# Block-sparse attention and a multiplicative FFN on one core: a new order of all engines and loads, paced loads, and pairs of heads taken by twos

## The chip, the cores and the metric

One NeuronCore of a Trainium2 chip. The metric is the device time of one execution in microseconds. The kernel before has a median of 254.29 us (254.08 to 254.67, three runs). The times that the chip reports are above the span of the same execution (254.47 against 252.7 in the profiled run of before), so spans are compared with spans and times with times.

## The reference, cut to what matters

```python
B, H, S, D = 4, 8, 768, 64                       # block = 32, 24 blocks
scores = scale * q @ k.T                         # per head
scores = where(mask, scores, -1e9)               # band, first and last block, 3 random blocks a row
attn   = softmax(scores);  x = attn @ v          # 3072 tokens x 512 after the heads are joined
a = x @ w1;  b = x @ w2                          # 512 -> 1024
out = ((a * b) @ w3) @ w_out                     # 1024 -> 1024 -> 512
```

Both kernels compute the product of w3 and w_out once (64 matmuls of 512 columns) and then two stages per 512 tokens: 64 matmuls for a and b, 32 for the output. There are six such FFN units.

## The kernel before

The kernel is a list of tasks with a duration, dependences and buffers. A small scheduler at build time plays the list through with modelled times, decides which task each engine takes next, and the instructions are then written in that order. The traces show each engine taking its instructions in that order, so a late input holds up what stands behind it on the same engine (TensorE's wait of 0.90 us ahead of its first FFN matmul, shown in the prediction, is one case).

```python
LOADS = ("a01 v00 v01 o0 o1 30 a02 v02 31 32 a03 v03 33 34 35 36 37 "
         "10 20 11 21 12 22 13 23 p10 p11 p12 p13 ...")   # a: q,k  v: v  o: w_out  3: w3  1,2: w1,w2  p: q,k,v
PRM = dict(bias=0.4, ..., vprio=1.5, w3prio=10.0, ..., trb=8, units="tttt", ...)
# (cut)
    def pick(self, eng, cands, free):                  # next task of an engine
        t0 = min(c[0] for c in cands)
        near = [c for c in cands if c[0] <= t0 + PRM["near"]]
        return min(near, key=lambda c: (c[1].prio, c[0]))
# (cut) keys and queries of the first trb pairs of heads: transposed on TensorE; later pairs: by DMA
            if (b, pr) in by_pe:
                # 12 nc.tensor.transpose each for q and k, then one eviction
            else:
                # a copy on VectorE, then nc.sync.dma_start(..., transpose=True)
# (cut) a tile of attention: 4 score matmuls, exp, mask multiply, 8 value matmuls
            prev_s = add(f"S {sk}", {PE: 0.216}, sc, ..., mode="S")
            exps.append(add(f"E {m} {j}", {ACT: 0.97}, ...))
# (cut) the FFN waits for x, which is transposed by DMA when all four pairs of a 256-token block are done
```

Two score buffers in PSUM limit how far TensorE can run ahead of ScalarE's exp. TensorE is kept busy at the start with matmuls on zeros ("spare"), so that its clock is up (in the trace of before the full clock is granted from 5.3 us on).

The softmax here doesn't subtract the row's maximum and nothing guards it: scores larger than these inputs give would overflow.

## Time and profile before

| | before |
|---|---|
| time, median | 254.29 us |
| span of the profile | 252.7 us |
| busy: TensorE, ScalarE, VectorE | 95%, 74%, 69% |
| first exp / first FFN matmul | 10.3 / 61.7 us |
| end of the last matmul to end of span | 4.0 us |

How to read it: with TensorE at 95% the question is not which engine is slow, but where TensorE has no useful work. The prediction below counts that. "Granted clock" is the share of its full clock that TensorE had.

### The profile page before, as it was taken

The page shows a single profiled execution, that of the slowest core. Times are in us where ns is not written, and L with a number is a line of the kernel's source. Part 1 is how long each engine was busy: PE and PEld are TensorE (multiplying, and loading weights), DVE is VectorE, ACT ScalarE, POOL GpSimd, SP SyncE. Part 2 cuts the span into 40 slices and gives each one's busy share as a digit, 9 for nine tenths or more (in the row PEclk, how much of TensorE's full clock was granted, in tenths as well). Part 3 has the DMA queues.
Part 4 walks back from the last instruction along what each step waited for, and adds up shares of the span by engine and source line. Part 5 has one row for each costly group of instructions (what it writes and reads, how often), then busy time and mean ns, then how long its engine had stood idle before and what let it go on. Part 6 is the DMA issues. An engine that isn't in the chain of part 4 may idle for free.

```text
span 252.7 us, 6330 instructions
## 1 busy us (share of the span) xinstructions
PE 240.6 (95%) x2647; PEld 130.5 (52%) x2689; DVE 174.9 (69%) x305; ACT 186.4 (74%) x231; POOL 44.9 (18%) x73
## 2 busy tenths in 40 slices
PE   7989999997999999999999999999999999999993
PEld 5554655664555455455455445555555554444441
DVE  5696698899699897988856776878777754312320
ACT  3685788897889898889888888788988862323321
POOL 8635455444421360000000000000000000000000
PEclk9999999999999999999999999999999999999998
DMA  7999999999997899994142020231201223022013
GB/s 174 171 205 207 208 210 194 164 199 167 177 173 99 104 144 194 184 242 86 34 110 101 4 42 3 61 108 44 42 4 21 65 89 79 0 83 83 4 42 125
DMA packets 45793, 28.08 MB, mean 111 GB/s; under 512 B 27332, under 2 KB 40644, under 8 KB 45764
## 3 DMA queue, kind: packets, MB, share of 16 engines
q0 software_dynamic: 15872, 14.29, 38.2%
q1 hardware_dynamic: 29892, 13.38, 25.4%
q8 instruction: 21, 0.34, 0.6%
q14 instruction: 8, 0.07, 0.1%
HBM read 29.36 MB, written 6.29 MB: 141 GB/s over the span
## 4 chain that ended last, share of the span: by engine, by line
PE 86%; DVE 4%; DMA 4%; ACT 3%; issue 2%; SPq 0%
PE f L622 33%; PE f L642 17%; PE s L528 14%; PE o L551 14%; PE f L603 5%; DMA x<-xn 4%; PE o L397 2%; DVE e L538 2%; ACT e L534 2%; PE f L474 1%; PE f L591 1%; DVE xn L561 1%; ACT qkt L293 0%; DVE w3t L293 0%; SPq L574 0%
## 5 line engine op out<-in xcount | busy, mean ns | idle before, releaser
L534 ACT ACTIVATE e<-s 128x1024 bf16<-128x1024 f32 x144 | 139.6, 1025 | 13.5 <-PE s L528 12.8
L622 PE MATMUL f<-x,w 128*128 128x512 bf16 x359 | 90.4, 379 | 2.8 <-issue 1.0
L538 DVE TENSOR_TENSOR e<-e,mask 128x2048 bf16<-128x2048 bf16 x72 | 87.4, 1218 | 7.4 <-ACT e L534 7.1
L551 PEld LDWEIGHTS <-e 128*128 128x128 bf16 x1152 | 44.1, 97 | 22.9 <-DVE xn L561 6.5
L633 DVE TENSOR_TENSOR big<-f,a 128x512 bf16<-128x512 f32 x48 | 33.1, 689 | 32.0 <-PE f L622 24.9
L551 PE MATMUL o<-v,e 128*128 128x65 bf16 x1152 | 50.6, 194 | 0.8 <-DVE xn L561 0.4
L622 PEld LDWEIGHTS <-w 128*128 128x128 bf16 x384 | 32.4, 98 | 35.3 <-issue 6.7
L642 PE MATMUL f<-wf,big 128*128 128x512 bf16 x183 | 46.2, 380 | 0.9 <-issue 0.6
L630 ACT CAST a<-f 128x512 bf16<-128x512 f32 x48 | 28.2, 588 | 24.6 <-PE f L622 24.6
L528 PE MATMUL s<-qkt 64*128 64x256 bf16 x576 | 45.2, 272 | 0.7 <-ACT e L534 0.7
L528 PEld LDWEIGHTS <-qkt 64*128 64x128 bf16 x576 | 22.2, 94 | 27.5 <-issue 24.1
L642 PEld LDWEIGHTS <-big 128*128 128x128 bf16 x192 | 16.1, 98 | 17.3 <-issue 3.2
L293 ACT COPY ob<-f 128x512 f32<-128x512 f32 x20 | 11.7, 587 | 14.1 <-PE f L642 14.1
L561 DVE TENSOR_TENSOR xn<-o,rec 128x256 bf16<-128x256 f32 x48 | 20.4, 424 | 1.7
L559 DVE RECIPROCAL rec<-o 128x4 f32<-128x4 f32 x48 | 8.6, 179 | 17.3 <-PE o L551 17.3
L603 PE MATMUL f<-wo,w3t 128*128 128x512 bf16 x56 | 15.8, 380 | 0.6 <-issue 0.3
L331 POOL DMA_DIRECT2D qn<-in_q_dram x15 | 10.9, 727 | 18.9 <-DVE qs L483 5.3
L331 POOL DMA_DIRECT2D kn<-in_k_dram x15 | 10.8, 719 | 14.1 <-DVE qs L483 6.2
L331 POOL DMA_DIRECT2D vn<-in_v_dram x16 | 11.4, 716 | 8.2 <-DVE v L496 5.8
L397 PE MATMUL o<-zero 128*128 128x256 bf16 (+1 forms) x45 | 7.8, 331 | 1.5 <-DVE zero L394 1.5
L293 DVE COPY qkt<-f 128x768 bf16<-128x768 bf16 x13 | 7.1, 552 | 2.0 <-PE f L474 1.9
L603 PEld LDWEIGHTS <-w3t 128*128 128x128 bf16 x64 | 4.9, 98 | 5.0 <-issue 0.6
(54 smaller groups left out, 87.1 us busy)
## 6 DMA issues: line engine op xcount, KB each, us to landing
out_dram<-ob SPq DMA_DIRECT2D x24, 256.0 KB, 2.0
vn<-in_v_dram POOLq DMA_DIRECT2D x16, 192.0 KB, 7.8
qn<-in_q_dram POOLq DMA_DIRECT2D x15, 192.0 KB, 8.1
kn<-in_k_dram POOLq DMA_DIRECT2D x15, 192.0 KB, 8.1
big<-in_moe_w_dram POOLq DMA_DIRECT2D x8, 256.0 KB, 8.9
w<-in_moe_w_dram POOLq DMA_DIRECT2D x8, 256.0 KB, 9.7
wo<-in_moe_w_out_dram POOLq DMA_DIRECT2D x2, 512.0 KB, 9.4
q<-in_q_dram SPq DMA_DIRECT2D x1, 384.0 KB, 3.2
```

The costliest lines, as they stand in the source:

```text
L293: (nc.scalar.copy if t.eng == ACT else nc.vector.tensor_copy)(out, in_)
L331: t = add(name, {POOL: 0.73}, lambda t: nc.gpsimd.dma_start(out=out_of(), in_=src), deps=deps, writes=writes, kind="load", prio=seq[0])
L528: nc.tensor.matmul(s[:, h, k2 * QT:(k2 + 1) * QT], lhsT=z[64 * h:64 * h + 64, 1, kc * 128:(kc + 1) * 128], rhs=z[64 * h:64 * h + 64, 0, t3 ...
L534: exps.append(add(f"E {m} {j}", {ACT: 0.97}, lambda t, sk=sk, ek=ek, j=j: nc.scalar.activation(T(*ek)[:, j], T(*sk), AF.Exp, scale=1.0 / 8 ...
L538: tm = add(f"K {m}", {DVE: 1.23}, lambda t, ek=ek, t3=t3, kp=kp: nc.vector.tensor_tensor(T(*ek), T(*ek), mask[:, t3, kp:kp + 2, :].unsquee ...
L551: nc.tensor.matmul(o[:, qt, h, :], lhsT=e[:, j, h, lo:lo + 128], rhs=w[:, h, kc, :], start=kc == 0 and qt == 0 and h == 0, stop=kc == C - ...
L561: tx = add(f"xn {rk}", {DVE: 0.42}, lambda t, rk=rk, ok=ok, xk=xk, pr=pr: nc.vector.tensor_tensor(T(*xk)[:, :, 128 * pr:128 * pr + 128].re ...
L603: nc.tensor.matmul(T(*key), lhsT=T("w3t", i)[:, j, :], rhs=wo_sb[:, j, :], start=j == 0, stop=j == NF - 1)
L622: nc.tensor.matmul(T(*key), lhsT=w[:, c, f * 128:(f + 1) * 128], rhs=T(*xk)[:, c, :], start=c == 0, stop=c == 3)
L630: ta = add(f"a {i}{f}", {ACT: 0.58}, lambda t, ak=ak, key=ends["w1"][0]: nc.scalar.copy(T(*ak), T(*key)), deps=[ends["w1"][1]], reads=[end ...
L633: nc.vector.tensor_tensor(T(*hk)[:, 512 * (f % 2):512 * (f % 2) + 512], T(*key), T(*ak), op=ALU.mult),
L642: nc.tensor.matmul(T(*key), lhsT=T(*hk[f // 2])[:, 512 * (f % 2) + n * 128:512 * (f % 2) + (n + 1) * 128], rhs=wf_sb[:, f, :], start=f == ...
```

## The change

The stated intent is an order that holds up under DMA delays. The scheduler's durations and its model of the DMA rings are refitted, its weights and the order of loads are searched for the mean time over replays with random delays, and some structure changes with it. The core of the diff, with cuts:

```diff
-LOADS = ("a01 v00 v01 o0 o1 30 a02 v02 31 32 a03 v03 33 34 35 36 37 "
-         "10 20 11 21 12 22 13 23 p10 p11 p12 p13 "
+LOADS = ("a01 30 a02 31 a03 v00 v01 36 o0 o1 v02 v03 32 35 33 34 37 20 10 22 p10 13 12 11 21 p11 "
+         "p12 23 p13 p20 p21 p22 p23 p30 p31 p32 p33")
-PRM = dict(bias=0.4, bmask0=1.0, bmask=1.0, btc=0.5, near=0.12, soon=0.06, kprio=2.0, eprio=0.5, aprio=1.0,
-           hprio=1.0, vprio=1.5, w3prio=10.0, ebufs=4, both=0.25, fo="31", pcopy=4.0, trb=8, units="tttt",
+PRM = dict(bias=0.102, bmask0=0.628, bmask=0.149, btc=-0.719, near=0.137, soon=0.0, kprio=3.289, eprio=0.296,
+           aprio=1.064, hprio=0.884, vprio=2.486, w3prio=28.201, ebufs=4, both=0.328, fo='31', pcopy=4.0,
+           trb=6, lead=9, slow=1.08, xeach=0.036, late=1.597, early=0.596, xlate=1.0, units='tQQQ', nat=4,
 ... first q and k: in halves, q from SP and k from ACT, cast and transposed by halves ...
+    def gate(b, pr):            # loads of batches 2 and 3 wait for a softmax reciprocal 9 units earlier
+            GATE[at] = add(f"gate {at}", {POOL: 0.2}, lambda t, rk=rk: nc.gpsimd.tensor_copy(
+                gate_sb, T(*rk)[:, 0, 0]), reads=[rk], prio=seq[0])
 ... opening zeros 128 instead of 256 columns wide while the clock is low ...
-        rows = 64 if mode == "S" else 128
+        rows, n = 64 if mode == "S" else 128, 128 if cold else 256
 ... the last output tile in two halves ...
+            width = d_model if 4 * i + n < 4 * NU - 1 else d_model // 2
```

`trb=6` sends pairs 2 and 3 of batch 1 through DMA transposes; `units='tQQQ'` takes the pairs of batches 1 to 3 two at a time.

## The prediction

> **What bounds the kernel now.** I read the page's busy shares first. TensorE is busy 95% of the span, against 74% for ScalarE and 69% for VectorE, and the granted clock is full. In the busy tenths the reader is to see that PE's first slices are the only ones under 9 besides the last: whatever can still be won lies in the first 60 us or so, and at the very end.
>
> ```profile
> span 252.7 us, 6330 instructions
> PE 240.6 (95%) x2647; PEld 130.5 (52%) x2689; DVE 174.9 (69%) x305; ACT 186.4 (74%) x231; POOL 44.9 (18%) x73
> PE   7989999997999999999999999999999999999993
> ```
>
> Second, the chain that ended last, in order of time. It is PE nearly throughout, and its pieces give the price of each kind of PE work.
>
> ```profile
> 1.47 5.41 PE o L397 x31
> 7.38 0.81 ACT qkt L293
> 8.23 0.86 PE f L474 x24
> 10.32 3.78 ACT e L534 x4
> 14.12 1.23 DVE e L538
> ...
> 175.48 0.73 PE o L551 x24
> 176.21 0.86 PE f L622 x4
> ...
> 201.34 0.54 PE s L528 x8
> 201.89 0.97 PE f L642 x4
> ...
> 241.92 6.92 PE f L642 x32
> 248.86 0.59 ACT ob L293
> ```
>
> A 512-column FFN matmul is 6.92 / 32 = 0.216 us. A value matmul (line 551) is 0.73 / 24 = 0.030. Eight score matmuls (528) are 0.54, of which the work is four pairs at 0.107 and the rest a change of array mode; the four FFN matmuls just after scores take 0.97 instead of 0.86, so leaving that mode costs another 0.1. Narrow transposes (474) are 0.86 / 24 = 0.036.
>
> Third, PE's timeline and its waits: where PE was not doing useful work.
>
> ```profile
> 1.47 5.41 PE L397 MATMUL o<-zero 128*128 128x256 bf16 x31 [1.47 <-DVE zero L394]
> 6.81 0.53 PE L474 MATMUL f<-ident,qn 128*64 128x128 bf16 x12
> ```
>
> ```profile
> PE f L622 <- DMA x<-xn: 0.9, 1, 0.9
> ```
>
> The 31 matmuls on zeros keep the clock up until data comes. But ScalarE had cast q by 3.92 + 0.83 = 4.75 us (its timeline), and the transposes started only at 6.81: the zeros ran 1.9 us too long. The last line is the first FFN matmul, which waits for transposed activations until 61.7 us.
>
> I add up the useful PE work from instruction counts and those prices: 640 FFN-size matmuls x 0.216 = 138.2; 1152 value matmuls x 0.0305 = 35.1; 288 score pairs x 0.107 = 30.8; 64 w3 transposes x 0.055 = 3.5; 192 narrow transposes x 0.028 = 5.4 between mode changes; masks 2.4; about 174 mode changes x 0.096 = 16.7. Sum 232.2. The span of 252.7 therefore holds 20.5 us without useful work. Where: 47.4 us of useful work stand ahead of the first FFN matmul at 61.7, so 14.3 are lost by then (6.8 before the first transpose, 1.6 for 14 later zero matmuls, 5.9 in waits). From 61.7 to PE's last matmul, ending 248.7, 187.0 us hold 184.8 of work: 2.2 lost, within the error of my prices. The tail from 248.7 to 252.7 is 4.0: cast, store, landing. 14.3 + 2.2 + 4.0 = 20.5.
>
> **What the Trainium skill says.** "TensorE: Matmul & The Clock Gate", under "What's actually happening", says that the array starts at half clock and needs about 3.4 us of activity to be released. The trace agrees: the 256-column zeros start 0.213 apart until 5.3 us and 0.109 after. So some zeros are needed, and their length should fit the time, not exceed it. "TensorEngine Tiling (Array Packing)" says, under "Key Properties", that changing the tiling mode drains the engine; the trace has 0.1 us per change, as above. "DMA: Bandwidth & Descriptors", under "Issuing engines are not separate DMA queues", says that transfers started from several engines run on the same 16 DMA engines and interleave. The trace agrees: while loads run, one activation transpose took 9.25 us on the chain; the fastest took 2.4.
>
> ```profile
> 52.34 9.25 DMA x<-xn
> ```
>
> ```profile
> DMA to landing us min/median/max: 2.4/4.0/10.5
> ```
>
> So pacing the loads can shorten those, but issuing the first k load from ScalarE only saves issue time (0.46 us).
>
> **The change part by part.** No arithmetic of the result changes; instructions move. The comparison of the programs' orders gives the counts.
>
> 1. Start. First q and k come in halves on two queues, are cast and transposed by halves, and the transposes take both heads at once. The first score group then needs only the first halves. Zeros before the first transposes fall to 30, now of 128 columns: cold at half of 0.213, 30 x 0.107 = 3.2 us, ending near 4.5. First useful work near 4.7 instead of 6.8: about -2.1. The first exp comes some 4 us earlier (near 6.2 instead of 10.3).
>
> 2. Zeros later: 26 after the first transposes instead of 14; some 26 x 0.1 = 2.6 against 1.6: +1.0. They stand where PE waits anyway, so they are a sign that 5 to 17 us stays thin.
>
> 3. Before the first value matmul the new order puts 9.3 us of useful work, the old 5.8: three more score tiles, more transposes, all masks. But v of the first pair is now seventh in the load queue and w_out eleventh. In the trace a 192 KB load lands about 1.0 us after the one before, a w3 block 1.2 and half of w_out 3. From the first landing at 6.5 us I estimate v at 16 and the second half of w_out at 22 to 23 (before: 9.7 and 16.7). ScalarE's chain gives the same time: ten exps at 0.93 plus eight evictions at 0.7 from 6.2 us end near 21. First w3·w_out product near 22.5 with 12.9 us of work done: 9.6 lost, against 10.0 before (18.9 with 8.9 done). So the earlier start gains only about 0.4 by this point; most is spent waiting for ScalarE and for v and w_out.
>
> 4. From there to the first FFN matmul the old order lost 14.3 - 10.0 = 4.3 us. The new order has 33.2 us of PE work there against about 25 exps x 0.92 plus 6 us of evictions = 29 on ScalarE, so PE can be dense; and it has ten more value tiles after the last that the first FFN input needs. I give it 1.7 lost. Gain 2.6.
>
> 5. 60 fewer narrow transposes on PE (pairs 2 and 3 of batch 1 go through DMA, first pair by twos): 60 x 0.036 = 2.1. Score groups stay at 76, so mode changes hardly change. On the bound engine this counts in full: -2.1.
>
> 6. Steady part: PE was already dense. Pairs by two and gated loads cannot gain here; they only must not lose. I set 2.6 lost against 2.2: +0.4.
>
> 7. The last output is cast and stored in two halves: half a cast (0.59 / 2) and a little of the store: -0.4.
>
> Sum over the span: -0.4 (1 to 3) - 2.6 - 2.1 + 0.4 - 0.4 = -5.1. Corrected for how far my reading of part 3 may be too strict (the load estimate uses a contended queue; the truth may be a microsecond better), -5.5. 254.3 - 5.5 = 248.8 us.
>
> **Rivals.** First, ScalarE becomes the bound. The new order leaves 244 FFN-size matmuls after the last value matmul, the old 188: 52.7 us against 40.6. So attention must be done in about 185 us instead of 196, with 166 us of ScalarE busy time in it: 90%. For: scores sit in pairs with two PSUM buffers, and 144 exps in the row of groups have a mean of 1.025 us; PE runs in fixed order, so a late exp stalls everything behind it. A stall of 0.05 us at each of 53 score groups is 2.7 us: 251.5. Against: exps that follow each other start 0.92 to 0.97 apart (3.78 for four), so the real load is lower.
>
> Second, a load takes the place of the wait. w_out later in the queue, or the gates, which tie batches 2 and 3 to a softmax reciprocal nine units earlier (some 34 us at 2.5 us per score group of two tiles). A late w_out would cost 2 or 3 us in one place: 251. The gates have so much lead against 9 us of landing that I expect nothing.
>
> Third, everything fits: PE starts at 4.7 and is filled by 15 us, with the losses before FFN at 9 instead of 11.3. That gives 246.5.
>
> Fourth, the order gains on a mean over delays, but this chip's delays are small (before runs within 0.6 us), so the robustness is not seen: then only parts 1, 5 and 7 count, about -3: 251.3.
>
> **Range and chances.** Two per cent is 5.1 us, that is 249.2. My sum lies at the edge of it: the sure parts (fewer transposes, tail, start) are 3 us, the rest depends on how densely PE is filled between 15 and 60 us. I put the 80% range at 246.2 to 251.7; faster by over 2% at 0.57, within at 0.42, slower at 0.01, since nothing adds work to PE.
>
> **What the profile after would show.** Right: transposes on PE starting before 5 us; first exp before 7; first FFN matmul at 56 to 59 us; PE's slices at 9 from the third on; no wait for x or exp over 0.5 us. Step 3 wrong if value matmuls start well before 16 us or w3·w_out waits on w_out. The ScalarE rival shows as PE waits for exp at line 624 spread over 60 to 190 us and the eights in PE's slices there. If the first FFN matmul is still later than 60 us, step 4 is wrong and the time stays above 250. If the first FFN is at 57 and the time still over 250, the steady part lost what the start gained.

## More of the kernel before

A view that the prediction did not show looks at ScalarE, which feeds TensorE with exps: between 10 and 30 us it works 14.58 of 20 us (columns: stretch, its length, then busy time and instruction count of TensorE, of its weight loads, of VectorE, ScalarE and GpSimd, then granted clock, DMA share, GB/s).

```profile
10.00:30.00 20.00, 18.52 (x239) 10.64 (x238) 15.21 (x30) 14.58 (x19) 8.57 (x15) 1.00 1.20 205
```

## The result, and the profile after

The changed kernel takes 247.21 us (247.11 to 247.40, four runs) against 254.24 in the same rounds: ratio 0.9722, 95% interval 0.9705 to 0.9739. A ratio here is the mean time of one kernel's fast runs over that of the other's fast runs of the same rounds, so it is not quite the ratio of the medians. Three executions of the later rounds that are slow (605.87 us of the kernel before, 258.94 of `b_cut`, 257.41 of `a_prm`) are left out of the ratios.

The page of the changed kernel: the span is 7.3 us shorter, and TensorE's first slices are full.

```profile
span 245.4 us, 6319 instructions
PE 240.5 (98%) x2648; PEld 131.5 (54%) x2648; DVE 175.8 (72%) x308; ACT 185.6 (76%) x232; POOL 46.6 (19%) x82
PE   8999999999999999999999999999999999999994
```

The busy time of TensorE is nearly the same (240.5 against 240.6), but the sum hides that the trace of before lacks 42 matmul records (2647 of 2689) and that of after none. TensorE's waits in the whole of the trace after are one line, the memset ahead of the first zero matmul; before there were ten.

```profile
PE o L478 <- POOL zero L475: 1.1, 1, 1.1
```

TensorE's timeline after (start, length, engine, line of the kernel, what is written from what, count; in brackets the idle time before it and what ended it), at the same places as before: transposes begin at 4.56 instead of 6.81, value matmuls at 18.56 instead of 14.87, the first FFN matmul at 56.10 instead of 61.72.

```profile
1.11 3.38 PE L478 MATMUL o<-zero 128*128 128x128 bf16 x30 [1.11 <-POOL zero L475]
4.56 0.50 PE L564 MATMUL f<-ident,q0n 128*128 128x128 bf16 x3
...
18.56 0.89 PE L647 MATMUL o<-v,e 128*128 128x65 bf16 x24
...
56.10 1.46 PE L721 MATMUL f<-x,w 128*128 128x512 bf16 x6
```

ScalarE in the stretch shown above for before: 18.13 of 20 us instead of 14.58. Sixteen exps are done at 30 us instead of ten.

```profile
10.00:30.00 20.00, 19.83 (x285) 12.23 (x282) 18.89 (x37) 18.13 (x23) 8.87 (x15) 1.00 1.22 206
```

The chain at the end: the last matmuls and a cast of half the width, 0.37 us instead of 0.59.

```profile
237.98 3.92 PE f L745 x26
241.90 0.03 ACTq L343
241.92 0.04 issue
241.96 0.37 ACT ob L343
```

Where the 7.4 us of span (252.71 to 245.35) went, counted as in the prediction (useful work from the orders: 232.2 before, 230.1 after):

| stretch | before | after | gain |
|---|---|---|---|
| start to the first w3 w_out product: time without useful work | 19.52 - 8.9 = 10.6 | 22.21 - 12.9 = 9.3 | 1.3 |
| from there to the first FFN matmul | 42.20 - 38.5 = 3.7 | 33.89 - 33.2 = 0.7 | 3.0 |
| from there to the last matmul's end | 186.9 - 184.8 = 2.1 | 185.6 - 183.9 = 1.7 | 0.4 |
| tail | 4.05 | 3.63 | 0.4 |
| useful work | 232.2 | 230.1 | 2.1 |

The sum is 7.2; the rest is rounding of my prices. Of the two gains of 0.4, that of the tail is read off the traces; that of the row above it is within what the prices can be off.

### The profile page after: what moved, and what is told of

The parts are those of the page before. It is cut to its first block, busy times and chain, and to the rows that moved or that the text cites. A ratio compares the mean times of both kernels' runs of the same rounds, so it can differ in the third digit from the quotient of the medians.

```text
span 245.4 us, 6319 instructions
## 1 busy us (share of the span) xinstructions
PE 240.5 (98%) x2648; PEld 131.5 (54%) x2648; DVE 175.8 (72%) x308; ACT 185.6 (76%) x232; POOL 46.6 (19%) x82
## 4 chain that ended last, share of the span: by engine, by line
PE 95%; ACT 2%; DVE 1%; POOL 0%; issue 0%; ACTq 0%; POOLq 0%
PE f L721 35%; PE f L745 17%; PE s L624 16%; PE o L647 16%; PE f L702 6%; PE f L690 2%; PE f L555 1%; PE o L478 1%; PE f L528 1%; ACT e L630 1%; PE f L564 1%; ACT qkt L343 1%; DVE hot L509 0%; DVE hot L507 0%; DVE q0n L343 0%
## 5 line engine op out<-in xcount | busy, mean ns | idle before, releaser
L630 ACT ACTIVATE e<-s 128x1024 bf16<-128x1024 f32 x144 | 140.8, 1030 | 13.6 <-PE s L624 12.2
L721 PE MATMUL f<-x,w 128*128 128x512 bf16 x384 | 94.0, 379 | 0.0
L647 PEld LDWEIGHTS <-e 128*128 128x128 bf16 x1152 | 43.4, 97 | 17.5 <-issue 4.0
L647 PE MATMUL o<-v,e 128*128 128x65 bf16 x1152 | 49.0, 194 | 0.0
L745 PE MATMUL f<-wf,big 128*128 128x512 bf16 (+1 forms) x200 | 46.8, 371 | 0.0
L745 PEld LDWEIGHTS <-big 128*128 128x128 bf16 x200 | 17.5, 98 | 17.6 <-issue 2.1
L343 ACT COPY ob<-f 128x512 f32<-128x512 f32 (+1 forms) x19 | 10.7, 564 | 16.1 <-PE f L745 16.1
L702 PE MATMUL f<-wo,w3t 128*128 128x512 bf16 x64 | 16.5, 380 | 0.0
L456 POOL COPY gate<-rec 128x1 f32<-128x1 f32 x8 | 1.4, 180 | 70.7 <-DVE rec L655 70.6
L478 PE MATMUL o<-zero 128*128 128x128 bf16 (+2 forms) x56 | 7.6, 297 | 1.1 <-POOL zero L475 1.1
(59 smaller groups left out, 98.1 us busy)
```

Of the source, the lines that this page charges most:

```text
L343: (nc.scalar.copy if t.eng == ACT else nc.vector.tensor_copy)(out, in_)
L630: exps.append(add(f"E {m} {j}", {ACT: 0.915}, lambda t, sk=sk, ek=ek, j=j: nc.scalar.activation(T(*ek)[:, j], T(*sk), AF.Exp, scale=1.0 / ...
L647: nc.tensor.matmul(o[:, qt, h, :], lhsT=e[:, j, h, lo:lo + 128], rhs=w[:, h, kc, :], start=kc == 0 and qt == 0 and h == 0, stop=kc == C - ...
L702: nc.tensor.matmul(T(*key), lhsT=T("w3t", i)[:, j, :], rhs=wo_sb[:, j, :], start=j == 0, stop=j == NF - 1)
L721: nc.tensor.matmul(T(*key), lhsT=w[:, c, f * 128:(f + 1) * 128], rhs=T(*xk)[:, c, :], start=c == 0, stop=c == 3)
L745: nc.tensor.matmul(T(*key)[:, :width], lhsT=T(*hk[f // 2])[:, at:at + 128], rhs=wf_sb[:, f, cols], start=f == 0, stop=f == NF - 1)
```

## The experiments

Twelve kernels, each against the kernel before in five rounds. Three chips were used; a variant of the changed kernel is best set beside the changed kernel's ratio (0.9722 or 0.9705), and its span beside 245.3 to 245.4. Each profile is of one execution; where that one lies at the edge of a wide run, the text says so. First, the changed kernel once more: 247.09 us, ratio 0.9705 (0.9683 to 0.9727), span 245.3.

> The changed kernel once more, unaltered, as the measure for the others of these rounds. Both theories: 247.2, span 245.4.

### Is TensorE the bound, or ScalarE?

```diff
+                        if i == 2 and part == 0:
+                            nc.tensor.matmul(T(*key), lhsT=w[:, 0, f * 128:(f + 1) * 128], rhs=T(*xk)[:, 0, :],
+                                             start=True, stop=True)
```

> The changed kernel with 16 superfluous 512-column matmuls in the third FFN unit, 3.45 us of TensorE work in the steady part, all orders else the same. Theory 1 (TensorE is the bound there, without slack): +3.4, 250.6, and ScalarE's idle time grows. Theory 2 (ScalarE paces it, TensorE hides some): under +2.

250.68 us against 247.09 in the same rounds: +3.6; span 249.5, +4.1. All 3.45 us of added work show, and a little more (the extra matmuls are closed groups of their own, overwritten at once; the profiled execution is the slowest of the five). ScalarE's busy time between 100 and 160 us falls from 55.10 to 52.80: there it had followed, not led. So the first rival of the prediction is refuted for this stretch, that of the third FFN unit; ahead of the first FFN matmul it was not tested in this way.

```profile
100.00:160.00 60.00, 60.00 (x746) 32.52 (x743) 52.71 (x92) 55.10 (x66) 10.20 (x18) 1.00 0.90 134
```

```profile
100.00:160.00 60.00, 59.14 (x716) 32.34 (x726) 50.64 (x87) 52.80 (x63) 10.94 (x19) 1.00 0.93 135
```

The first line is the changed kernel, the second the one with the extra matmuls (42 matmul records are missing from that trace as from that of before, so its PE column is a little low).

### The start alone, in the old order

```diff
+    zeros = [t for t in log if t.name == "spare"][16:31]
     for t in log:
-        t.go(t)
+        if not any(t is z for z in zeros):
+            t.go(t)
```

> The kernel before with 15 of its 31 opening zero matmuls left out, every other instruction in the same order. Theory 1 (the zeros overran by 1.9 us, but what follows soon waits for the k cast, ScalarE and loads): first transposes near 5.0 instead of 6.8, first exp near 8.9 instead of 10.3, first FFN matmul 0.6 to 1.2 us earlier, time 253.3. Theory 2 (the start counts in full, since TensorE is the bound): 252.3. Theory 3 (all of it is absorbed by later waits): 254.2.

Transposes begin 1.8 us earlier, the first exp 0.8 (9.50 against 10.32), the first FFN matmul 0.77 (60.95), and the span is 0.7 shorter. The timeline shows the first thief: TensorE now waits a microsecond for the block mask, which hangs on the random-block indices.

```profile
5.00 0.85 PE L474 MATMUL f<-ident,qn 128*64 128x128 bf16 x12
6.80 0.49 PE L435 MATMUL f<-hot,Ab 24*24 24x512 bf16 x2 [0.96 <-DVE Ab L423]
```

The times do not resolve so little: ratio 0.9997, interval 0.9958 to 1.0036 (255.09 against 254.62 us), which leaves room for a gain of up to 1 us. The profiled execution, 253.72 us, is one of the two fastest. So in the old order an earlier start by 1.8 us is worth 0.7 us by the trace, and nothing that the times show.

### The start alone, in the new order

```diff
-        rows, n = 64 if mode == "S" else 128, 128 if cold else 256
+        rows, n = 64 if mode == "S" else 128, 256
```

> The changed kernel with its early zeros 256 columns wide again instead of 128; all orders the same. First transposes near 6.4 instead of 4.56. Theory 1 (ScalarE is busy without a gap from the first exp to the first w3 product, so a late first exp shifts all of it): +1.3 to +1.8, time 248.8. Theory 2 (the wait for v and w_out hides it): under +0.5.

```profile
1.10 6.30 PE L478 MATMUL o<-zero 128*128 128x256 bf16 x30 [1.10 <-POOL zero L475]
7.25 0.33 PE L564 MATMUL f<-ident,q0n 128*128 128x128 bf16 x3
```

The transposes start 2.7 us late (more than I had expected, because the clock stayed low until 7.0 us in this run), value matmuls 2.2, the first FFN matmul 2.1, the end of the span 2.1. Time 248.68 us, ratio 0.9758 against 0.9722 and 0.9705: 0.9 to 1.4 us by the ratios. The trace has more because its execution, 249.25 us, is the slowest of the five. So in the new order a late start is passed on, in this trace 2.1 of 2.7 us, against 0.7 of 1.8 in the old order. That fits a start which counts when ScalarE has scores to work on once it has begun, but this reason is argued, and the times alone, with their intervals, do not separate the two cases.

### The order of loads, and the weights of the search

One run sets back the order of loads and the scheduler's weights together, one only the order of loads. Both are planned anew, so every engine's order moves with them. Structure (halves at the start, DMA transposes, gates, pairs by twos, split store) and the refitted durations stay in both.

```diff
-LOADS = ("a01 30 a02 31 a03 v00 v01 36 o0 o1 v02 v03 32 35 33 34 37 20 10 22 p10 13 12 11 21 p11 "
-         "p12 23 p13 p20 p21 p22 p23 p30 p31 p32 p33")
+LOADS = (as before)
-PRM = dict(bias=0.102, bmask0=0.628, bmask=0.149, btc=-0.719, near=0.137, soon=0.0, kprio=3.289, eprio=0.296,
-           aprio=1.064, hprio=0.884, vprio=2.486, w3prio=28.201, ebufs=4, both=0.328, ...
+PRM = dict(bias=0.4, bmask0=1.0, bmask=1.0, btc=0.5, near=0.12, soon=0.06, kprio=2.0, eprio=0.5,
+           aprio=1.0, hprio=1.0, vprio=1.5, w3prio=10.0, ebufs=4, both=0.25, ...      (this part in a_prm only)
```

> The changed kernel with the twelve weights of the scheduler and the order of loads set back to those of the kernel before; structure and durations of the model stay new. Theory 1 (the searched order earns its part between 15 and 56 us): first FFN matmul 2 us later, time 249.2, later part as dense. Theory 2 (structure and better durations are all of it): 247.2 within 0.5.

With both set back the gain is gone: 254.98 us, ratio 1.0005 (0.9934 to 1.0075). Transposes do start at 4.56 and the first exp at 6.58, yet the first FFN matmul comes at 59.82, of which only 45.6 is useful work: 14.2 us lost, as in the kernel before (14.3). Both theories are missed: the better of them put 249.2. From the first FFN matmul to the end another 2.7 us go against the changed kernel (191.95 against 189.25), where theory 1 had that part as dense. TensorE waits again, mostly for exps: three of these waits are ahead of the first FFN matmul, two, 1.0 us together, near 100 us. The profiled execution, 253.54 us, is the fastest of five fast ones that reach 256.7.

```profile
PE s L625 <- ACT e L631: 2.8, 5, 0.9
...
PE o L648 <- DVE v L596: 0.7, 1, 0.7
```

> The changed kernel with only the order of loads set back to the old one, planned anew with the new weights (useful work +0.7 us by its orders). Theory 1 (load order and weights belong together; the run with both set back lost all of the gain, mostly ahead of the first FFN matmul, and the load order is what decides there): first FFN matmul after 58, 250 to 253. Theory 2 (the weights decide, the load order is free): 248.0.

With the loads alone set back: 252.07 us, ratio 0.9901 (0.9880 to 0.9922), first FFN matmul at 60.82 us. That is theory 1. Nearly all of the 5 us stand ahead of that matmul (4.8 against the repeat of the changed kernel); by its orders 0.7 us is more useful work. The mechanism is on ScalarE, between 10 and 30 us:

```profile
10.00:30.00 20.00, 19.04 (x232) 11.47 (x234) 13.76 (x28) 13.33 (x19) 8.49 (x16) 1.00 1.20 203
```

```profile
13.97 0.58 ACT L344 CAST mask<-f 128x512 bf16<-128x512 f32 x1
18.42 1.07 ACT L344 COPY w3t<-f 128x512 bf16<-128x512 bf16 x2 [3.86 <-PE f L691]
19.38 0.82 ACT L344 COPY qkt<-f 128x768 bf16<-128x768 bf16 x1
```

After six exps, those of the first two pairs, ScalarE has nothing to do: with v and w_out ahead in the queue, q of the third pair lands only at 18.47 us in this trace (18.87 in the kernel before), against 11.38 in the changed kernel. The next exp starts at 22.56. In the changed kernel q and k of the next pairs come first, v lands at 16.56 and w_out at 21.34 and 25.02, and ScalarE runs almost without a gap from 7 us on. Exps done at 30 us: 10 before, 10 with the old loads, 11 with loads and weights old, 16 in the changed kernel.

So, with the rest of the change in place, the order of loads, and the plan that follows from it, is worth 2.0% (0.9901 to 0.9705, same rounds) and the weights, given the old loads, about 1.0% (1.0005 to 0.9901, different chips, so less sure). The new loads with the old weights cannot be had: the scheduler then gets stuck over buffers. How far each weight counts stays open.

### Transposes through DMA

Back on TensorE for pairs 2 and 3 of batch 1, in the changed kernel:

```diff
-           trb=6,
+           trb=8,
```

> The changed kernel with pairs 2 and 3 of batch 1 transposed on TensorE again (48 transposes more, no DMA transposes for them), planned anew. Theory 1 (TensorE is dense, each transpose counts): useful work +1.7 us by its orders, time 248.9, TensorE without gaps after 20 us. Theory 2 (transposes fill waits): within 0.4 of 247.2.

248.84 us, ratio 0.9765; first FFN matmul at 56.06, no waits after 20 us: +1.7 us in the median and +1.8 in span, as the count of 48 transposes says (1.1 to 1.5 by the ratios, which come from different chips). The same step in the other direction, in the kernel before (`trb=8` to `trb=6`):

> The kernel before with pairs 2 and 3 of batch 1 transposed by DMA, planned anew by its own scheduler: 48 transposes fewer, useful work -1.4 us by its orders. Theory 1 (counts in full): 252.9. Theory 2 (the old loads, without order or pacing, slow the DMA transposes, so that TensorE waits for qkt): no gain or slower, 254 to 256.

265.89 us, ratio 1.0408: theory 2, and 10 us worse than its range (the profiled execution, 267.89 us, is the slowest of six). The chain shows transposes of 11 us, and TensorE waits 3 us for tiles of attention. Between the two stands VectorE: its copies for later transposes wait 12.0 us in all for these to land, and its multiplies by the mask come late behind them.

```profile
75.75 11.09 DMA qkt<-qs
...
89.45 11.53 DMA qkt<-qs
```

```profile
98.18 0.62 PE L551 MATMUL o<-v,e 128*128 128x65 bf16 x8 [3.01 <-DVE e L538]
...
102.05 0.62 PE L551 MATMUL o<-v,e 128*128 128x65 bf16 x8 [2.71 <-DVE xn L561]
```

```profile
PEclk9999999999999985599999999999999999999999
DMA  7999999999999999066148202024030140213003
```

The old order of loads alone is not the cause, though it is the obvious suspect: the two runs with the old loads in the new kernel have the same 20 transposes through DMA, and the slowest of them landed 7.6 and 7.7 us after their issue, against 14.9 here. What they have and this run lacks are the gates (below), the refitted durations and the pairs by twos. Without gates the slowest took 12.2 us in the changed kernel, which cost it only 0.7 us. So pacing seems to keep the transposes short, and the plan decides what late ones cost; which part of the plan stays open.

The last two lines carry a second lesson. The DMA engines are full until about 106 us, and in slices 15 to 17 the granted clock falls to half: in the trace it is at half from 98.1 to 111.8 us, 13.7 us long. If TensorE had had work all that time, half clock cost it up to 6.8 us (an estimate, half of 13.7) of the 13.4 us of span by which this trace is longer than that of before. The Trainium skill, "TensorE: Matmul & The Clock Gate", under "HAM oscillation — how this bites in real kernels", warns of such re-throttling after gaps over some 3.4 us; here the clock fell at the end of a wait of 3.0 us, with TensorE busy in 0.47 of the 3.4 us before.

All of batch 1 through DMA, in the changed kernel (`trb=4`), the one variant that the counts said might beat both:

> The changed kernel with all pairs of batch 1 transposed by DMA (48 transposes fewer, useful work -1.2 us by its orders), planned anew. Theory 1 (with paced loads the DMA transposes come in time): 246.0, faster than both kernels. Theory 2 (the first transposes of batch 1 fall among the weight loads, before any gate, and land late): waits for qkt of 2 to 10 us before 80 us, 249 or more.

259.1 us, ratio 1.0183 (1.0142 to 1.0224). The time is that of theory 2, but no wait of TensorE for keys and queries is seen. The transposes for batch 1 fall before any gate, and they share one queue with the x transposes, which then come late.

```profile
53.77 0.41 PE L647 MATMUL o<-v,e 128*128 128x65 bf16 x8 [1.09 <-DVE xn L660]
54.90 0.81 PE L647 MATMUL o<-v,e 128*128 128x65 bf16 x16 [0.72 <-DVE e L634]
58.15 2.29 PE L721 MATMUL f<-x,w 128*128 128x512 bf16 x5 [2.44 <-DMA qn<-in_q_dram]
```

The view names a q load, but no q load landed then; in the trace the last x transpose, issued at 44.41, landed at 58.06, just ahead of the matmul, so that is what it waited for. In the changed kernel the same transpose, with none of batch 1 issued ahead of it, was issued at 43.98 and landed at 53.85: 9.9 us instead of 13.7. The clock fell to half here too, for 6.8 us, and already at 55.24, before the wait of 2.44 us began: two waits of 1.09 and 0.72 us, with TensorE busy in 1.55 of the last 3.4 us, had gone ahead. The first FFN matmul is only 2 us late; of the remaining 9 us of span some 2 are FFN matmuls at half clock until 62.1 and 3.6 are waits of 0.1 to 0.5 us for exps and VectorE between 92 and 107 us. Why the new plan is thin there was not looked into.

### Pacing, pairs by twos, the split store

```diff
     for t in log:
-        t.go(t)
+        if not t.name.startswith("gate"):
+            t.go(t)
```

> The changed kernel without the eight gate instructions that pace the loads of batches 2 and 3; all other orders the same. Theory 1 (pacing gives nothing on the chip once the order is fixed, since the transposes land well before their readers): 247.2 within 0.4. Theory 2 (unpaced loads slow the DMA transposes that TensorE reads): waits of TensorE for x or qkt, over +1.

248.19 us, ratio 0.9739 (0.9709 to 0.9769), span 246.0, all orders the same. One wait appears, ending at 95.74 us, with the two x transposes landing at 95.19 and 95.61 instead of 90.47 and 91.74.

```profile
PE f L721 <- DMA x<-xn: 0.7, 1, 0.7
```

So pacing is worth 0.7 us by the trace and 0.4 to 0.9 by the ratios, whose intervals overlap with that of the changed kernel: the trace has more than the nothing of theory 1 and less than theory 2, the times alone cannot tell.

Four pairs at a time in all batches (`units='tttt'`), planned anew:

> The changed kernel with heads of batches 1 to 3 taken four pairs at a time again, planned anew. By its orders 82 score groups instead of 76, useful work +1.1 us. Theory 1 (mode changes count, nothing else): 248.3. Theory 2 (pairs by two is what keeps the order dense, their keys would come late): waits of TensorE for qkt, over 250.

250.09 us, ratio 0.9791 (0.9738 to 0.9845), span 248.1, +2.7. Of this 1.1 is the mode changes of 82 score groups instead of 76, and 1.5 are waits near 88 to 92 us, for exps and VectorE. The result lies between the two theories, and nothing waits for qkt.

The last tile whole:

```diff
-            width = d_model if 4 * i + n < 4 * NU - 1 else d_model // 2
+            width = d_model
```

> The changed kernel with the last output tile cast and stored whole. Theory 1: the tail from the last matmul to the end grows from 3.6 to 4.0, time +0.4, 247.6. Theory 2: the store's fixed time hides it, +0.1 or less.

```profile
237.94 3.68 PE f L745 x17
241.62 0.02 issue
241.64 0.58 ACT ob L343
```

The cast takes 0.58 instead of 0.37 and the tail grows from 3.6 to 4.2 us, while the matmuls end 0.2 to 0.3 us earlier in this trace. Time 247.44 us, ratio 0.969 with a wide interval (0.9636 to 0.9744; three of the runs of before in these rounds lie above 257). The time can't tell; the tail of the trace says 0.5 us or less. No variant beat the changed kernel clearly, and none tested the halves at the start apart from the zeros.

## Why the prediction was right or wrong

The time, 247.2, lies in the range of 246.2 to 251.7, and faster by over 2% had the larger chance. The expected gain was 5.5, the measured 7.0. Term by term, what was off was off on the same side, so no two errors cancelled.

- What bounds the kernel: right. The run with 16 superfluous matmuls pays for all of them. (TensorE's slices before show one more dip than the first ones and the last, a 7 at 57 to 63 us, around its wait for x.)
- Steps 1 to 3, the start to the first w3 w_out product: predicted 0.4, measured 1.3. The times were close (transposes predicted at 4.7, seen at 4.56; first product 22.5, seen 22.21; second half of w_out 22 to 23, landed at 25.02). Two thirds of the difference (0.6) are a misreading: I took 18.9 us for the first product of before, where ScalarE's eviction starts; the product is at 19.52. The same 0.6 was then counted in step 4, so the sum did not suffer. The first exp came at 7.02 in the profiled run, later than the 6.2 of step 1 and just past the sign set for it (6.69 in the repeat). In the queue v is the ninth load and w_out the twelfth, not the seventh and eleventh; the times were right all the same. My view of the late v and w_out was one-sided: I counted what they delay, and missed that the same order feeds ScalarE, which is where the next step's gain comes from.
- Step 4, from there to the first FFN matmul: predicted 2.6, measured 3.0. Without the misreading of 0.6 it would have been 2.0. The reason, that TensorE can be dense because ScalarE keeps up, fits the trace, where no wait is left; the order loses 0.7 us there instead of the 1.7 that I gave it, and this is the largest error. (The 5.9 us "in waits" ahead of the first FFN matmul of before were a remainder: the trace names about 3.4 of them.) First FFN matmul at 56.1, at the near edge of my 56 to 59.
- Step 5, fewer transposes: 2.1. The run with 48 of them back on TensorE costs 1.7, as counted; the other 12 have no run of their own.
- Step 6, the steady part: this term was mis-sized too. I set a loss of 0.4; it gained 0.4, though losses of 2.1 and 1.7 us are both within the error of my prices. I took stalls for likely since the new order asks more of ScalarE; the trace has none. My "cannot gain, only must not lose" holds against the kernel before, which was dense here; but in the new order the gates keep 0.7 us of span and the pairs by twos 2.7 (1.1 of it mode changes) that would be lost without them.
- Step 7, the tail: predicted 0.4, measured 0.4.
- The rivals: ScalarE as the bound is refuted by the extra matmuls, for the stretch where they stand. The late w_out did land 2 us later than I reckoned, and no wait came of it. The third, that everything fits, came closest: 246.5 us, with 9 us lost ahead of the first FFN matmul, where 10.0 were. The fourth, that only the sure parts count and the order's robustness is not seen, is the most wrong: with the old loads and weights the sure parts are all still there, and the gain is nil.

What I had not seen is that the parts are not additive. The start by itself is worth 0.7 us by the trace in the old order and some 2 in the new (nothing, and about 1, by the times); 48 transposes moved to DMA gain 1.7 us in the new plan and cost 4% in the old.

## What to carry to other kernels

When the busiest engine is nearly full, count useful work by instruction and look for the stretch where it and its feeder are both thin; feed the feeder first, here q and k for ScalarE's exps ahead of v and w_out, even though the value matmuls then start 3.7 us later. Moving work from a full engine to DMA pays only if the loads leave room for it and the plan allows for it: test it together with their pacing and a new plan. And a structural improvement tried without a new order may show nothing, so do not throw it out on that evidence alone.

## What the Trainium skill lacked or had wrong

- "TensorE: Matmul & The Clock Gate", "Back-to-back issue gap": it gives about 131 ns per 512-column matmul and 81 ns per 128-column one as the sustained pace of pairs of weight load and matmul, and calls 216 ns the isolated one. In these runs the sustained pace is 216 ns (64 in 13.81 us in the changed kernel's chain, each with its weight load), and that of the 128-column w3 transposes about 55 ns (12 in 0.67 us in the chain of before). The page's isolated figures are the ones that held.
- The same page, "What you observe": it puts the release of the clock around 4 us into sustained matmuls, give or take half a microsecond. The zeros here start at 1.1 to 1.5 us, and in the fourteen traces the clock was released at 3.9 to 7.0 us, that is 2.8 to 5.9 us after the first of them; between two traces of the very same program (the changed kernel, 6.0 and 6.8) lie 0.8 us. A note under "What's actually happening" does say that it varies between runs.
- "HAM oscillation — how this bites in real kernels", same page: its rule is no idle gaps over some 3.4 us. Here one wait of 3.0 us in a thin stretch, and in another run two of 1.09 and 0.72 us, came ahead of half clock, which then lasted 13.7 and 6.8 us. TensorE was busy in 0.47 and 1.55 of the 3.4 us before; in the twelve traces that kept the clock no stretch of 3.4 us between 10 us and the last matmul has under 2.0 us of work. So the busy share of a stretch is to be watched, and not the longest gap alone.
- "TensorEngine Tiling (Array Packing)", "Key Properties", says that a mode change drains the array, and gives no time: about 0.1 us each way here, 15 us in all over 76 score groups (an estimate, 2 x 76 x 0.1).
- "DMA: Bandwidth & Descriptors" gives a bandwidth for a transposing transfer, but no time to landing among loads: 2.4 us at the fastest here, up to 14.9 with the DMA engines full, and its issue on SyncE up to 5.1 us instead of 1.2.
